# Gated linear attention followed by a two-layer network: step 2's loads placed behind the transfers into x, and the attention set at other units

## The chip, the cores and the metric

The kernel runs on 1 core of one Trainium2 chip. The metric is the device time of one execution in microseconds; the time given for the kernel before is the median of 3 runs. Shorter is better.

## The reference

For batch 4, 8 heads, 768 positions and a head size of 48, a state of 48 by 48 is carried along the positions; its 384 outputs per position then go through a two-layer network of width 2048.

```python
f = 1.0 / (1.0 + np.exp(-f_logit))
for t in range(S):
    state = f[:, :, t, :, None] * state + np.einsum('bhd,bhe->bhde', k[:, :, t], v[:, :, t])
    y[:, :, t] = np.einsum('bhd,bhde->bhe', q[:, :, t], state)
x = y.transpose(0, 2, 1, 3).reshape(B * S, H * D)
h = x @ w_in
g = np.where(h >= 1, h, np.where(h <= -1, 0.0, (h + 1) ** 2 / 4))
return g @ w_out
```

Inputs and outputs are float32.

## The kernel before, in words

The 768 positions are cut into 6 steps of 128 (step i = 0 to 5), all four batches at once, so that a step has 512 columns. In each step the attention gives x, 384 rows in three tiles `x[:, t]`, each as a rounded high part and a low part. The network then runs over 16 blocks j of 128 hidden rows.

**Units.** One block j of one step, 512 columns wide, is a unit. `unit_1` multiplies x by `w_in`: 9 matmuls into `ph` (high weight by both parts of x, then low weight, line 230). Its activation is made by ScalarE twice (lines 233 and 236), VectorE (line 241), ScalarE (rounding to `ghi`, line 244) and VectorE (the rest `glo`, line 247). `unit_2` multiplies by `w_out`: 9 matmuls into `po` (line 254). On TensorE `unit_2` of a unit comes after `unit_1` of the next. Units 0 to 15 are step 0. Step 1 starts in halves of 256 columns: units 16 to 19 are its first half of columns over blocks 0 to 7, two blocks each, units 20 to 23 the second half over the same blocks, and units 24 to 31 its blocks 8 to 15 at full width. From unit 32 on each step has 16 full units.

**Attention of a step.** It goes by four pairs of heads, n = 4i to 4i + 3. `gate` loads k and q (`in_kq`, 512 KB, line 267 through `dma`) and the gate logits (`in_f`), takes the sigmoid on ScalarE (line 443), runs two scans over the positions on VectorE (lines 445 and 452) and scales k and q (lines 454 and 456). `scores` is 16 matmuls of 128 columns (line 561) and a mask on VectorE (line 568). `outputs` (lines 622 and 630) gives two pairs of heads, rounded by ScalarE and VectorE (lines 600 and 601); `states` (line 670) carries the state on. The fourth pair's heads are made in a tile `y3` and moved into the three tiles of x by six small transfers, three on SyncE's queue (SP) and three on ScalarE's (line 272). `unit_1` of the step's first unit reads those rows. For step 1 this happens twice, once for each half of the columns; `moved[1, 1]` are the six transfers of its second half, which unit 20 reads.

**Weights.** They come as 64-bit words, in 24 pieces of 512 KB (`in_w`), and are put together by three VectorE operations each (`split_piece`, lines 335, 338 and 340) and split into a high and a low part, `w_hi` and `w_lo`. For 9 pieces, named by `moving`, the low part is made by ScalarE (line 345) and a transfer from GpSimd's queue that adds (line 346); for the other 15 by VectorE (line 350). Pieces are taken in the order `order[k]`: three of `w_in`, three of `w_out`, and so on, each group of six serving four units. All 24 pieces are read a second time later (`small_piece`, one reduction on VectorE each, line 358), only for a test on their size.

**What sets the order.** Every operation is given to a `Plan` with a cost and what it depends on; `Plan.order` then sorts all of them by a list schedule with these costs, and the engines get their instructions in that order. Dependencies in the plan set the order alone: the semaphores that an instruction waits for follow from the tiles that it reads and writes. Where the plan leaves TensorE idle for over 500 ns, `warm` puts in matmuls on zeros (line 308). `AT` and the table in the main loop say at which unit each `scores` (first list) and `outputs` (second list) is given to the plan.

Of the kernel before, what the change touches and what calls it, by code (L numbers as in the profile page):

```python
# [37 lines left out]
NT = 3  # L38

W = 512  # L40
NW = DM * DF // (128 * W)
# [99 lines left out]
def gla_moe(ctx: ExitStack, tc: tile.TileContext, ff, kqd, f0, vv, vad, vbd, wd, maskd, identd, gates, values, headsd, out):  # L141
# [30 lines left out]
    raw = tiles(3, [128, W], I64, "raw")  # L172
# [25 lines left out]
    HALVES = 1  # L198
# [67 lines left out]
    def dma(dst, src, kb, *deps):  # L266
        return add("SP", "issue", lambda: nc.sync.dma_start(dst, src), *deps, kb=kb)
# [46 lines left out]
    piece = []  # L314
# [9 lines left out]
    def split_piece(k):  # L324

        c = order[k]
        lw, hw = words_of(raw[k % 3])

        moving = k in (4, 6, 9, 10, 11, 12, 17, 19, 23)
        t = bits[k % 4]  # L330
        val = t.bitcast(F32)
        loaded = dma(raw[k % 3], wd[c], 8 * 128 * W / 1024, piece[k - 3] if k >= 3 else None)


        m = vec("words", lambda: nc.vector.tensor_scalar(
            out=t, in0=hw, scalar1=3, scalar2=0x3FFFFFF8, op0=ALU.logical_shift_left, op1=ALU.bitwise_and),
            loaded, split[order[k - 4]] if k >= 4 else None)
        v = vec("dve", lambda: nc.vector.scalar_tensor_tensor(  # L338
            out=t, in0=lw, scalar=29, in1=t, op0=ALU.logical_shift_right, op1=ALU.bitwise_or), m)
        v = vec("dve", lambda: nc.vector.scalar_tensor_tensor(  # L340
            out=t, in0=hw, scalar=0xC0000000, in1=t, op0=ALU.bitwise_and, op1=ALU.bitwise_or), v)
        piece.append(v)
        if moving:

            n = sca("copy", lambda: nc.scalar.activation(w_lo[:, c], val, AF.Copy, scale=-1.0), v)
            l = add("POOL", "swdge", lambda: nc.gpsimd.dma_start(w_lo[:, c], val, accum_op=ALU.add), n, kb=560)
            h = sca("copy", lambda: nc.scalar.copy(w_hi[:, c], val), v)
        else:
            h = sca("copy", lambda: nc.scalar.copy(w_hi[:, c], val), v)
            l = vec("dve", lambda: nc.vector.tensor_tensor(out=w_lo[:, c], in0=val, in1=w_hi[:, c].bitcast(F32), op=ALU.subtract), h)  # L350
        split[c] = [h, l]

    seen = []

    def small_piece(c):

        loaded = dma(raw[2], wd[c], 8 * 128 * W / 1024, seen[-1:] or piece[-3:])
        seen.append(vec("dve", lambda: nc.vector.tensor_reduce(
            out=ok[:, 1 + NG + c:2 + NG + c], in_=words_of(raw[2])[1].bitcast(F32), axis=mybir.AxisListType.X, op=ALU.min,
            apply_absolute_value=True), loaded))  # L360
# [30 lines left out]
    att = [None] * len(pairs)  # L391
# [4 lines left out]
    def old(n, *names, of=att):  # L396

        return [] if n < 0 else [of[n].get(k) for k in names]
# [7 lines left out]
    def gate(m, halves=(None,)):  # L406

        i, p = divmod(m, NT)
        t = kq[p]
        split_up = i == HALVES  # L410

        ft, before = (f[m], None) if m < 2 else (act_f[1], None) if m == 2 else (f[(m - 1) % 2], m - 3 if m < 5 else m - 2)
        et = end[m % 2]
        steps = ((0, 2), (2, 4)) if m == 0 or split_up else ((0, 4),)
        count = len(steps)
        if gates_of[m] is None:
            c = gates_of[m] = {k: [] for k in ("km", "qm", "sg", "en", "s2", "lf", "pf")}
            if not split_up:
                c["lk"] = dma(t[:, 0:2 * N], kqd[i, p], 512, [old(NP * i - k, "sc", "y", "tr") for k in ((1, 2, 3, 4) if i == HALVES + 1 else (NP - p,))],
                              old(m - NT, "km", "qm", "to", of=gates_of))  # L420
            else:
                c["lk"] = dma(t.rearrange("r (h c) -> r h c", h=2)[:, :, 0:N], kqd[i, p].rearrange("r (h c) -> r h c", h=2), 512,
                              old(NP * (i - 1) + p, "sc", "y", "tr"), old(m - NT, "km", "qm", "to", of=gates_of))
        c = gates_of[m]
        if m == 0:
            ready["mask"] = dma(mask, maskd, 64)
            ready["f0"] = sca(200, lambda: nc.scalar.activation(f0s, f0s, AF.Sigmoid), dma(f0s, f0, 36))
        lk = c["lk"]
        for h, (b0, b1) in enumerate(steps):
            if split_up and h not in halves:  # L430
                continue
            o = h if split_up else None

            shift = 1 if split_up and h else 0
            cols = slice(b0 * C + (1 if b0 and not split_up else 0) + shift, b1 * C + 1 + shift)
            l = dma(ft[:, cols], ff[i, p, :, cols], 256 // count, of_half(before, o, "qm") if before is not None else None)
            last = of_half(m - 1, o, "km", "en", "s2")
            u0, u1 = B - b1, B - b0
            fwd = ft[:, b0 * C + shift:b1 * C + shift]
            bwd = ft[:, b1 * C + shift:b0 * C + shift:-1]  # L440
            kt, qt = (t[:, HW * h:HW * h + HN], t[:, HW * h + HN:HW * h + 2 * HN]) if split_up else (
                wide(part(t, 0)[:, u0:u1]), wide(part(t, 1)[:, b0:b1]))
            sg = sca("sig" if count == 1 else 420, lambda cols=cols: nc.scalar.activation(ft[:, cols], ft[:, cols], AF.Sigmoid), l)  # L443

            s1 = vec(1200 // count, lambda bwd=bwd, u0=u0, u1=u1: nc.vector.tensor_tensor_scan(  # L445
                out=wide(w[:, u0:u1]), data0=bwd, data1=wide(ones[:, u0:u1]), initial=0.0,
                op0=ALU.mult, op1=ALU.add), sg, None if split_up else c["sg"], set_ones, last)
            en = vec("small", lambda b0=b0, b1=b1, u0=u0, u1=u1: nc.vector.tensor_scalar(
                out=et[:, b0:b1], in0=w[:, u1 - 1:(u0 - 1 if u0 else None):-1, C - 1], scalar1=1e-30, scalar2=None, op0=ALU.max),
                s1, of_half(m - 2, o, "pf"))  # L450
            rc = vec("small", lambda b0=b0, b1=b1: nc.vector.reciprocal(out=rec[:, b0:b1, 0], in_=et[:, b0:b1]), en, last, set_rec)
            s2 = vec(1200 // count, lambda fwd=fwd, b0=b0, b1=b1: nc.vector.tensor_tensor_scan(  # L452
                out=fwd, data0=fwd, data1=wide(rec[:, b0:b1]), initial=0.0, op0=ALU.mult, op1=ALU.add), rc, s1)
            km = vec(620 // count + 60 * (count - 1), lambda kt=kt, u0=u0, u1=u1: nc.vector.tensor_tensor(
                out=kt, in0=kt, in1=wide(w[:, u0:u1]), op=ALU.mult), s1, lk)
            qm = vec(620 // count + 60 * (count - 1), lambda qt=qt, fwd=fwd: nc.vector.tensor_tensor(
                out=qt, in0=qt, in1=fwd, op=ALU.mult), s2, lk)
            for name, d in (("sg", sg), ("en", en), ("km", km), ("qm", qm), ("s2", s2)):
                c[name].append(d)
            if split_up:  # L460
                least(m, h, t[:, HW * h + 2 * HN:HW * (h + 1)], et[:, b0:b1], f0s[:, m * B + b0:m * B + b1], en)
        if not split_up:
            least(m, None, whole(t), et, f0s[:, m * B:m * B + B], c["en"])
# [27 lines left out]
    def elementwise(n):  # L491
# [14 lines left out]
        if by_half:  # L506
            k = p % 2
            if h == 0:
                c["lv"] = dma(v[k], vv[i, k], 384, before, att[2]["st"])
            else:  # L510
                c["lv"] = att[n - 2]["lv"]
        elif n % 2:
            c["lv"] = att[n - 1]["lv"]
        elif i == 0:
            c["lv"] = dma(va if p == 0 else vb, vad if p == 0 else vbd, 512 if p == 0 else 640)
        else:
            c["lv"] = dma(v[k], vv[i, p // 2], 384, before, att[2]["st"])
        if NP - 1 in mine:

            every = range(NT * i, NT * i + NT)  # L520
# [318 lines left out]
        x_of[0, t] = rounded(firsts[t][0], wide(firsts[t][1]), x[0][:, t, 0], x[0][:, t, 1], y, None)  # L839
    for k in range(2 * NW):  # L840
        split_piece(k)
    for c in range(2 * NW):
        small_piece(c)

    BY_TENSOR = 2
    groups = {}

    AT = [5, 9, 16, 17], [10, 18]
    for n in range(NP, len(pairs)):
        i, m = divmod(n, NP)  # L850
        u = NJ * (i - 1)
        groups.setdefault(AT[0][m] if i == 1 else u + ((3, 4, 12, 13) if i == 2 else (-1, 0, 5, 10))[m], []).append((0, n))
        if m % 2 == 0:
            groups.setdefault(AT[1][m // 2] if i == 1 else u + ((7, 14) if i == 2 else (2, 13))[m // 2], []).append((1, n))
    for u in range(len(order_of)):
        unit_1(u)
        if u == 0:
# [15 lines left out]

        if 1 <= u < len(order_of) - 2:
            unit_2(u - 1)
    test()
    for u in range(len(order_of) - 3, len(order_of)):
        unit_2(u)
# [151 lines left out]
```

## Time and profile before

| | |
|---|---|
| runs | 511.97, 511.47, 509.25 us; median 511.47 us |
| the profiled execution | 514.73 us, of which the span from first to last instruction is 513.0 us |
| busy: TensorE | 498.4 us, 97% |
| busy: VectorE | 378.7 us, 74% |
| busy: ScalarE | 233.7 us, 46% |
| mean granted TensorE clock | 0.991 |
| DMA | 56.67 MB, mean 110 GB/s |

PE is TensorE, DVE VectorE, ACT ScalarE, POOL GpSimd and SP SyncE; a q behind a name is that engine's queue, where DMAs are issued. Times are microseconds from the span's start. In a timeline a row has start, length, engine, line, operation and tiles, and xN where N instructions are merged; in brackets stands the idle time of the engine just before and what ended it. Matmuls overlap each other, so that the distance between two starts says more than a length, and a busy PE is not one at its peak.

### The profile page before, as it was taken

The numbers are of one execution on the slowest core, as the hardware profiler recorded it, in microseconds if no ns is written. First come the engines' busy times: TensorE is split into PE (matmuls) and PEld (weight loads), VectorE is DVE, ScalarE is ACT, GpSimd is POOL, SyncE is SP. The second block draws the span as 40 slices with busy tenths as digits, with TensorE's granted clock in tenths as the row PEclk, the third lists the DMA queues.
The fourth block names the chain that finished last, engine by engine and source line by source line (L and its number), as shares of the span: only waits on it lengthen the run. The fifth ranks groups of instructions, "written<-read, shape, count | busy, mean of one in ns | idle before, by whom it ended". The sixth has DMA issues, their size and how long they took to land.

```text
span 513.0 us, 8673 instructions
## 1 busy us (share of the span) xinstructions
PE 498.4 (97%) x3412; PEld 406.1 (79%) x3412; DVE 378.7 (74%) x751; ACT 233.7 (46%) x386; POOL 31.9 (6%) x62
## 2 busy tenths in 40 slices
PE   8999999999799999999999999999999999999994
PEld 3677788789799877877888788788788888888883
DVE  7999999998689998999948999845755443433332
ACT  2266756653244443434543443543444444544441
POOL 2101301110100020101100010100000000000000
PEclk9999999999799999999999999999999999999999
DMA  8878947346504005230226150136533101100001
GB/s 314 248 242 280 251 143 203 115 124 211 186 2 145 1 21 145 108 99 0 74 92 165 66 183 18 46 124 174 184 125 123 42 1 31 64 0 1 0 1 67
DMA packets 21840, 56.67 MB, mean 110 GB/s; under 512 B 3456, under 2 KB 5120, under 8 KB 21792
## 3 DMA queue, kind: packets, MB, share of 16 engines
q1 hardware_dynamic: 19152, 51.51, 30.2%
q0 software_dynamic: 1296, 2.36, 2.6%
q10 hardware_dynamic: 1344, 2.17, 1.8%
q8 instruction: 29, 0.48, 0.4%
q14 instruction: 19, 0.16, 0.1%
HBM read 44.61 MB, written 4.72 MB: 96 GB/s over the span
## 4 chain that ended last, share of the span: by engine, by line
PE 53%; DVE 30%; DMA 9%; issue 3%; ACT 2%; SPq 1%; ACTq 0%; DVEq 0%
PE po L254 25%; PE ph L230 24%; DVE kn L595 7%; DVE act L241 3%; DVE glo L247 3%; DMA kq<-in_kq 3%; DVE am L568 3%; DVE bits L338 2%; PE pa L561 2%; DMA raw<-in_w 2%; DVE w L445 2%; DVE bits L340 2%; DVE f L452 2%; DMA v<-in_v 2%; DMA f<-in_f 2%
## 5 line engine op out<-in xcount | busy, mean ns | idle before, releaser
L230 PE MATMUL ph<-x,w_hi 128*128 128x512 f32 (+1 forms) x618 | 148.6, 376 | 3.2 <-DMA kq<-kq 3.1
L230 PEld LDWEIGHTS ph<-x,w_hi 128*128 128x128 f32 x618 | 111.8, 191 | 24.3 <-ACT ghi L244 3.3
L241 DVE SCALAR_TENSOR_TENSOR act<-ph,act 128x512 f32<-128x512 f32 x96 | 65.9, 687 | 79.9 <-ACT act L236 79.4
L233 ACT ACTIVATE act<-ph,half 128x512 f32<-128x512 f32 x96 | 66.0, 687 | 126.1 <-PE ph L230 110.3
L244 ACT CAST ghi<-act 128x512 fp32r<-128x512 f32 x96 | 59.5, 620 | 100.9 <-DVE act L241 95.9
L254 PE MATMUL po<-ghi,w_hi 128*128 128x512 f32 (+1 forms) x312 | 87.8, 388 | 1.0 <-ACT ghi L244 0.7
L247 DVE TENSOR_TENSOR glo<-act,ghi 128x512 fp32r<-128x512 f32 x96 | 65.8, 686 | 24.9 <-ACT ghi L244 23.7
L254 PE MATMUL po<-glo,w_hi 128*128 128x512 f32 (+1 forms) x312 | 83.6, 374 | 0.0
L254 PE MATMUL po<-ghi,w_lo 128*128 128x512 f32 (+1 forms) x312 | 83.6, 374 | 0.0
L230 PE MATMUL ph<-x,w_lo 128*128 128x512 f32 (+1 forms) x309 | 82.4, 375 | 0.7 <-DMA w_lo<-bits 0.7
L254 PEld LDWEIGHTS po<-ghi,w_hi 128*128 128x128 f32 x312 | 53.4, 188 | 15.4 <-ACT ghi L244 4.2
L230 PEld LDWEIGHTS ph<-x,w_lo 128*128 128x128 f32 x309 | 56.5, 191 | 11.3 <-DMA w_lo<-bits 1.1
L254 PEld LDWEIGHTS po<-glo,w_hi 128*128 128x128 f32 x312 | 55.6, 188 | 11.4 <-DVE glo L247 0.9
L254 PEld LDWEIGHTS po<-ghi,w_lo 128*128 128x128 f32 x312 | 55.9, 188 | 10.7
L236 ACT ACTIVATE act<-act 128x512 f32<-128x512 f32 x96 | 60.7, 632 | 4.0 <-issue 1.1
L595 DVE STREAM_TRANSPOSE kn<-kq 32x128 f32<-32x128 f32 x192 | 58.1, 302 | 2.8
L568 DVE TENSOR_TENSOR am<-pa,mask 128x512 f32<-128x512 f32 x46 | 30.2, 681 | 4.2 <-PE pa L561 4.2
L561 PEld LDWEIGHTS pa<-kq 48*128 48x128 f32 x368 | 24.1, 193 | 6.9 <-issue 5.0
L561 PE MATMUL pa<-kq 48*128 48x128 f32 x368 | 28.8, 291 | 0.0
L445 DVE TENSOR_TENSOR_SCAN w<-f,ones 128x512 f32<-128x512 f32 (+1 forms) x21 | 21.2, 1014 | 2.1 <-ACT f L443 2.1
L452 DVE TENSOR_TENSOR_SCAN f<-f,rec 128x512 f32<-128x512 f32 (+1 forms) x21 | 21.3, 1019 | 0.6
L443 ACT ACTIVATE f<-f 128x513 f32<-128x513 f32 (+2 forms) x21 | 11.3, 547 | 22.1 <-DMA kq<-kq 9.3
(88 smaller groups left out, 350.3 us busy)
## 6 DMA issues: line engine op xcount, KB each, us to landing
raw<-in_w SPq DMA_DIRECT2D x48, 512.0 KB, 3.9
kq<-in_kq SPq DMA_DIRECT2D x18, 512.0 KB, 5.3
out_y<-raw SPq DMA_DIRECT2D x18, 256.0 KB, 2.7
v<-in_v SPq DMA_DIRECT2D x10, 384.0 KB, 6.0
f<-in_f SPq DMA_DIRECT2D x13, 256.5 KB, 3.2
w_lo<-bits POOLq DMA_DIRECT2D x9, 256.0 KB, 5.0
kq<-kq SPq DMA_DIRECT2D x15, 64.2 KB, 4.8
kq<-kq ACTq DMA_DIRECT2D x15, 64.2 KB, 4.6
```

The costliest lines, as they stand in the source:

```text
L230: nc.tensor.matmul(ps[:, to], w_in(w_hi if high else w_lo, j, kt), xt[:, kt, t, c], start=(n == 0), stop=(n == 8))
L233: nc.scalar.activation(a, ps, AF.Relu, bias=half, scale=0.5)
L236: nc.scalar.activation(a, a, AF.Square)
L241: nc.vector.scalar_tensor_tensor(out=a, in0=ps, scalar=1.0, in1=a, op0=ALU.max, op1=ALU.min)
L244: nc.scalar.copy(hi, a)
L247: nc.vector.tensor_tensor(out=lo, in0=a, in1=hi.bitcast(F32), op=ALU.subtract)
L254: nc.tensor.matmul(po[e][:, c], w_out(part, j, e), g[:, of], start=(j == 0 and n == 0 and c.start == 0), stop=(j == NJ - 1 and n == 2))
L445: s1 = vec(1200 // count, lambda bwd=bwd, u0=u0, u1=u1: nc.vector.tensor_tensor_scan(out=wide(w[:, u0:u1]), data0=bwd, data1=wide(ones[:, ...
L452: s2 = vec(1200 // count, lambda fwd=fwd, b0=b0, b1=b1: nc.vector.tensor_tensor_scan(out=fwd, data0=fwd, data1=wide(rec[:, b0:b1]), initia ...
L561: nc.tensor.matmul(ps[:, m], key(n, q, b)[a:z], query(n, q, b)[a:z], start=True, stop=True)
L568: o = vec("dve", lambda t=t, ps=ps: nc.vector.tensor_tensor(out=t, in0=ps, in1=mask.rearrange("u (o t) -> u o t", o=1).broadcast_to([C, B, ...
L595: nc.vector.transpose(kn[n % 2][u:u + 32, ::-1, r:r + 32], src[:, :, u:u + 32])
```

## The change

Five things change. The loads of k and q for step 2 (`ahead` in `gate`) and every load of v from step 2 on (`elementwise`) get the six transfers `moved[1, 1]` as a dependency in the plan. So does the second reading of the weights (`small_piece`), which is also given to the plan after all units but the last instead of before the first. The list `moving` names other pieces, again 9. And the units at which scores and outputs are placed are others, for all of steps 1 to 5.

```diff
-        moving = k in (4, 6, 9, 10, 11, 12, 17, 19, 23)
+        moving = k in (4, 5, 7, 10, 11, 13, 17, 20, 21)
...
-        loaded = dma(raw[2], wd[c], 8 * 128 * W / 1024, seen[-1:] or piece[-3:])
+        loaded = dma(raw[2], wd[c], 8 * 128 * W / 1024, seen[-1:] or [piece[-3:], moved[HALVES, 1]])
...
+            ahead = moved[HALVES, 1] if i == HALVES + 1 else None
...
-                              old(m - NT, "km", "qm", "to", of=gates_of))
+                              old(m - NT, "km", "qm", "to", of=gates_of), ahead)
...
-            c["lv"] = dma(v[k], vv[i, p // 2], 384, before, att[2]["st"])
+            c["lv"] = dma(v[k], vv[i, p // 2], 384, before, att[2]["st"], moved[HALVES, 1])
...
-    AT = [5, 9, 16, 17], [10, 18]
+    AT = [3, 7, 14, 16], [10, 17]
...
-        groups.setdefault(AT[0][m] if i == 1 else u + ((3, 4, 12, 13) if i == 2 else (-1, 0, 5, 10))[m], []).append((0, n))
+        groups.setdefault(AT[0][m] if i == 1 else u + ((5, 8, 10, 12) if i == 2 else (-1, 2, 6, 8))[m], []).append((0, n))
...
-            groups.setdefault(AT[1][m // 2] if i == 1 else u + ((7, 14) if i == 2 else (2, 13))[m // 2], []).append((1, n))
+            groups.setdefault(AT[1][m // 2] if i == 1 else u + ((9, 13) if i == 2 else (4, 11))[m // 2], []).append((1, n))
```

Two lines are added ahead of the rest, so that from line 420 on a line of the changed kernel has a number higher by 2.

First, SP's queue around the transfers of step 1's second half into x (`x_86<-y_87`), before. `raw_92` and `raw_93` hold outputs of step 0, `kq_68` to `kq_70` get step 2's k and q, `raw_94` the second reading of the weights.

```order
L267 DMA out_y<-raw_93 128x512
L267 DMA raw_94<-in_w 128x512
L267 DMA kq_68<-in_kq 128x1024
L267 DMA kq_69<-in_kq 128x1024
L267 DMA kq_70<-in_kq 128x1024
L267 DMA v<-in_v 128x768 x2
L267 DMA raw_94<-in_w 128x512
L272 DMA x_86<-y_87 16x2x256 x3
L267 DMA f_67<-in_f 128x513
```

The same place of SP's queue in the changed kernel:

```order
L267 DMA out_y<-raw_93 128x512
L272 DMA x_86<-y_87 16x2x256 x3
L267 DMA kq_68<-in_kq 128x1024
L267 DMA kq_69<-in_kq 128x1024
L267 DMA v<-in_v 128x768
L267 DMA kq_70<-in_kq 128x1024
L267 DMA v<-in_v 128x768
L267 DMA raw_94<-in_w 128x512
L267 DMA f_67<-in_f 128x513
```

Seven large loads that stood ahead of SP's three transfers into x stand behind them or later. None of them has a semaphore of those transfers to wait for that it did not have: it is the place in the queue that changes.

Second, VectorE between line 241 of unit 12 (`act_83`) and of unit 13 (`act_84`), before:

```order
L241 SCALAR_TENSOR_TENSOR act_83<-ph_111,act_83 128x512
L350 TENSOR_TENSOR w_lo<-bits_96,w_hi 128x512
L338 SCALAR_TENSOR_TENSOR bits_98<-raw_94,bits_98 128x512
L247 TENSOR_TENSOR glo_90<-act_83,ghi_88 128x512
L340 SCALAR_TENSOR_TENSOR bits_98<-raw_94,bits_98 128x512
L350 TENSOR_TENSOR w_lo<-bits_97,w_hi 128x512
L601 TENSOR_TENSOR x_86<-pa_109,x_86 112x2x256
L241 SCALAR_TENSOR_TENSOR act_84<-ph_112,act_84 128x512
```

And in the changed kernel, without the first of these rows (lines 603, 456 and 458 are 601, 454 and 456 of before):

```order
L335 TENSOR_SCALAR bits_97<-raw_93 128x512
L603 TENSOR_TENSOR x_86<-pa_109,x_86 112x2x256
L247 TENSOR_TENSOR glo_90<-act_83,ghi_88 128x512
L458 TENSOR_TENSOR kq_68<-kq_68,f_66 128x256
L456 TENSOR_TENSOR kq_69<-kq_69,w 128x256
L458 TENSOR_TENSOR kq_69<-kq_69,f_67 128x256
L338 SCALAR_TENSOR_TENSOR bits_97<-raw_93,bits_97 128x512
L681 TENSOR_TENSOR sd<-pa_108,sd 112x4x96
L603 TENSOR_TENSOR x_86<-pa_110,x_86 112x256
L603 TENSOR_TENSOR y_87<-pa_110,y_87 112x256
L340 SCALAR_TENSOR_TENSOR bits_97<-raw_93,bits_97 128x512
L241 SCALAR_TENSOR_TENSOR act_84<-ph_112,act_84 128x512
```

Step 1's gates for its second half (456 and 458) and the rounding of its first half moved in ahead of unit 13's activation; two splits on line 350 moved out from between.

Third, TensorE in unit 12 (`ph_111<-x_85`) in the changed kernel, from its high weights to its low ones; before, the two L230 rows follow each other.

```order
L230 MATMUL ph_111<-x_85,w_hi 128x512 x6
L308 LDWEIGHTS zeros
L308 MATMUL po_115<-zeros 128x512
L308 LDWEIGHTS zeros
L308 MATMUL po_115<-zeros 128x512
L308 LDWEIGHTS zeros
L308 MATMUL po_115<-zeros 128x512
L308 LDWEIGHTS zeros
L308 MATMUL po_115<-zeros 128x512
L308 LDWEIGHTS zeros
L308 MATMUL po_115<-zeros 128x512
L230 MATMUL ph_111<-x_85,w_lo 128x512 x3
```

Five matmuls on zeros are put in there, and four more at the same place of unit 4; three that stood between units 5 and 6 are gone. In all there are 69 instead of 63.

More of the change, by code (lines that the diff above doesn't have):

```diff
@@ L841, in gla_moe @@
         split_piece(k)
-    for c in range(2 * NW):
-        small_piece(c)
     BY_TENSOR = 2
     groups = {}
-    AT = [5, 9, 16, 17], [10, 18]
+    AT = [3, 7, 14, 16], [10, 17]
     for n in range(NP, len(pairs)):
@@ L875, in gla_moe @@
             unit_2(u - 1)
+    for c in range(2 * NW):
+        small_piece(c)
     test()
```

## The prediction

> **What bounds the kernel now.** I read the page's head first, for the busy time of each engine and the strip of the clock.
>
> ```profile
> PE 498.4 (97%) x3412; PEld 406.1 (79%) x3412; DVE 378.7 (74%) x751; ACT 233.7 (46%) x386; POOL 31.9 (6%) x62
> PEclk9999999999799999999999999999999999999999
> ```
>
> PE is busy for 97% of the span, so that only what adds, removes or slows its work counts. In the strip one slice has a 7 where all others have a 9. The waits of PE (total, times, longest) say where it stands idle:
>
> ```profile
> PE ph L230 <- DMA kq<-kq: 3.1, 1, 3.1
> PE ph L308 <- DVE zeros L280: 1.7, 1, 1.7
> ...
> PE ph L230 <- DMA w_lo<-bits: 0.7, 1, 0.7
> ```
>
> One wait of 3.1 us stands out. PE's timeline around it shows the place:
>
> ```profile
> 126.83 0.88 PE L230 MATMUL ph<-x,w_hi 128*128 128x256 f32 x6
> ...
> 129.08 1.16 PE L561 MATMUL pa<-kq 48*128 48x128 f32 x16
> 130.17 0.98 PE L254 MATMUL po<-ghi,w_hi 128*128 128x256 f32 x6
> ...
> 135.68 1.84 PE L230 MATMUL ph<-x,w_hi 128*128 128x256 f32 x6 [3.08 <-DMA kq<-kq]
> ...
> 142.01 0.98 PE L254 MATMUL po<-ghi,w_hi 128*128 128x256 f32 x6
> ```
>
> The waiting matmuls read x, and they are unit 20's, the first of step 1's second half. PE had nothing to do from 135.68 − 3.08 = 132.60. Behind the wait, the same five groups (four of line 230, one of 561) that took 130.17 − 126.83 = 3.34 us at 126.83 take 142.01 − 135.68 = 6.33 us. Of the wait's 3.08 us the clock thus makes 3.08 + 2.99, about 6.1.
>
> The wait's releaser is given as a transfer `kq<-kq`, but what unit 20 reads is x. So I looked at SP's queue (start, length of the issues) around `moved[1, 1]`, with the first half's transfers for comparison, and at VectorE's row that makes y3 ready:
>
> ```profile
> 99.95 2.30 SPq L272 DMA_DIRECT2D x<-y  x3
> ...
> 121.47 1.34 SPq L267 DMA_DIRECT2D kq<-in_kq  x3
> 124.23 1.15 SPq L267 DMA_DIRECT2D v<-in_v  x2
> 125.48 0.51 SPq L267 DMA_DIRECT2D raw<-in_w  x1
> 127.56 4.26 SPq L272 DMA_DIRECT2D x<-y  x3
> ```
> ```profile
> 125.81 0.42 DVE L601 TENSOR_TENSOR y<-pa,y 112x256 fp32r<-112x256 f32 x1
> ```
> ```profile
> DMA to landing us min/median/max: 2.1/3.5/8.0
> ```
>
> y3 is ready at 125.81 + 0.42 = 126.23, SP issues its three transfers from 127.56 to 131.82, in 4.26 us against 2.30 for the first half, and the last row (tile x, SP's transfers) gives 3.5 us as their median from issue to landing. 131.82 + 3.5 = 135.3 meets PE's 135.68. Six large loads were issued in the 6 us before.
>
> The engine next to full is VectorE. Its share by stage (PE, PEld, DVE, ACT, POOL busy, then clock, DMA share, GB/s):
>
> ```profile
> 50.00:100.00 50.00, 49.90 (x321) 40.60 (x322) 49.28 (x97) 33.39 (x58) 8.47 (x11) 1.00 0.61 182
> 125.00:150.00 25.00, 21.91 (x169) 20.94 (x168) 17.78 (x39) 6.75 (x11) 1.31 (x2) 0.86 0.43 140
> 150.00:250.00 100.00, 99.41 (x758) 82.41 (x757) 95.66 (x216) 43.10 (x70) 7.82 (x12) 1.00 0.22 69
> ```
>
> From 50 to 100 VectorE has 0.7 us free in 50: whatever is put earlier in its order there makes something else later. From 125 to 150 it has 7.2 us free; the clock there is 0.86.
>
> **The change part by part.**
>
> *The x transfers.* Two things bring them forward. Large loads no longer stand ahead of SP's three, which should take the first half's 2.30 us. And the outputs go from unit 18 to 17, so that VectorE rounds y3 earlier: by order, one unit's operations of lines 241 and 247 and three small readings less stand ahead of it.
>
> ```profile
> L358 DVE TENSOR_REDUCE ok<-raw 128x1 f32<-128x512 f32 x24 | 16.4, 683 | 4.4 <-DMA raw<-in_w 4.3
> ```
>
> With the row's 683 ns for all five, which work on as many elements, that is 3.4 us; I take 3.0, since such operations overlap a little. y3 is then ready at 123.2, the issues end at 123.2 + 0.1 + 2.3 = 125.6, and x lands at 129.1 with the median of 3.5, at 133.6 with the greatest landing of 8.0. PE comes to unit 20 at 132.60, less the scores that move from unit 19 to 21 (129.08 to 130.17, 1.1 us), plus the 2.6 us by which it will be late (below): 134.1. The wait goes, with either landing. **−3.1 us for the wait, −3.0 us for the clock.** What is late next is nothing of x.
>
> *Warm matmuls and w_lo.* Nine are added, three taken away. Their price, and the piece transfers of line 346 with what unit 12 reads:
>
> ```profile
> 54.84 0.82 PE L308 MATMUL po<-zeros 128*128 128x512 bf16 x3
> 55.50 0.55 PE L581 MATMUL pa<-ident,kq 112*128 112x112 f32 x4
> ```
> ```profile
> 84.17 0.86 POOL L346 DMA_DIRECT2D w_lo<-bits  x1 [2.12 <-ACT w_lo L345]
> ```
> ```profile
> 90.97 0.84 PE L230 MATMUL ph<-x,w_lo 128*128 128x512 f32 x3
> ```
> ```profile
> DMA to landing us min/median/max: 3.8/5.0/7.9
> ```
>
> Three take 0.66 us from start to start, so six more are 1.3. Four of the nine take the place of the 0.7 us wait on `w_lo` at unit 4 (in the waits above): net +0.6. At unit 12 the low weight that arrives by transfer is piece 20's instead of 19's; issued about 1.5 us later than 84.17 (two and a half VectorE operations later by order), it lands at 89.5 to 93.6, against 90.97 plus five warm matmuls, 92.1. That is −0 to +1.5 us, median none.
>
> *Gates ahead of activations.* This is the part that costs. Of the second half's gates and rounding, by the order shown for VectorE, everything that ran from the first row 601 of 256 columns to unit 15's activation now stands ahead of unit 13's activation. In before:
>
> ```profile
> 94.33 0.68 DVE L241 SCALAR_TENSOR_TENSOR act<-ph,act 128x512 f32<-128x512 f32 x1
> ...
> 98.54 0.68 DVE L241 SCALAR_TENSOR_TENSOR act<-ph,act 128x512 f32<-128x512 f32 x1
> 99.14 0.41 DVE L601 TENSOR_TENSOR x<-pa,x 112x256 fp32r<-112x256 f32 x1
> ...
> 106.83 0.68 DVE L241 SCALAR_TENSOR_TENSOR act<-ph,act 128x512 f32<-128x512 f32 x1
> ```
> ```profile
> 99.25 0.62 ACT L244 CAST ghi<-act 128x512 fp32r<-128x512 f32 x1 [0.51 <-DVE act L241]
> ```
> ```profile
> 100.25 0.84 PE L254 MATMUL po<-ghi,w_hi 128*128 128x512 f32 x3
> ```
>
> Unit 13's is the row at 98.54. From 99.14 to 106.83 are 7.7 us; less three operations of the units themselves at 0.60 from start to start (98.54 to 99.14), 5.9. What moved out from ahead is one piece's three operations and two splits, five at 0.60 or a little less: 3.0. Unit 13's activation comes 2.9 us later by that. PE reads that unit's `ghi` at 100.25, 1.71 behind the row at 98.54; the activation (0.68) and ScalarE's rounding (0.62) with the passing on between them fill some 1.4 of that, so that 0.3 us is spare. PE is then 2.6 us late behind unit 13. The 0.6 us of warm matmuls and a wait for `w_lo` at unit 12 lie inside these 2.6, since PE would wait for VectorE anyway: the larger counts, not the sum. Later units gain nothing back on PE, which is full. **+2.6 us**; the ends are +0.6, if the order's extra work fits into pauses that I don't see, and +3.9, if nothing was spare and unit 15 sets it, ahead of which about 1 us more stands by order than ahead of unit 13.
>
> *Step 2's loads.* k and q go behind x.
>
> ```profile
> kq<-in_kq SPq DMA_DIRECT2D x18, 512.0 KB, 5.3
> ```
>
> Issued from 125.6 on instead of 121.47, and 5.3 us under way, they land some 4 us later, the first near 131, and VectorE waits that much for it. Their scores, however, go from unit 19 to unit 21, two units or 8 us later (94.33 to 98.54 is one), and VectorE has 7.2 us free there: nothing; with the cover gone at most the 4. The small readings that go back from here (four of them past 255 us, 2.7 us of VectorE) go to a stage where it has room; with them and the gates that moved, VectorE has about 3.6 us less ahead of unit 41 than before by order, which matches PE's gain. Nothing; if they collide, up to +2.
>
> The sum is −3.1 − 3.0 + 2.6 = **−3.5 us**. The profiled execution took 514.73 us (1.7 beside the span), so 511.2 by its own time. The median of the runs is 511.47, 3.3 under it; I take the difference over: **508.0 us**.
>
> **The rivals.**
>
> *The clock did not drop in ordinary runs (0.15).* The three runs spread from 509.25 to 511.97, 2.7 us, as much as the half clock costs, and the profiled one lies above them all; the two upper ones speak for a drop in most. Then only 3.1 goes and 2.6 comes: −0.5, 511.0. [...]
>
> *Slower: VectorE stops PE long enough (0.14).* If unit 13's lateness falls on PE in one piece of 3.1 us, the half clock moves from unit 20 to unit 13: 3.9 late there and 3.0 for the clock. Against it: 0.6 of it is filled by warm matmuls, and the 1.7 us wait above has no 7 in the strip. [...] Where the runs of before had the drop, this is −6.1 + 6.9 = +0.8; where they hadn't, −3.1 + 6.9 = +3.8, **515.3**. [...]
>
> *VectorE takes it back later (0.08).* At 95.66 of 100 us from 150 to 250 it follows PE closely; PE coming 3.5 us earlier may find activations unfinished. Against it stands the work moved back. Then about −0.5, 511.0.
>
> *The change doesn't do what it says (0.05).* No semaphore is added; ScalarE's three transfers into x keep their queue. If those are the late ones, and y3 is not earlier because VectorE is 2.9 us late, the wait stays and 2.6 comes: 514.1.
>
> **How the numbers follow.** The forecast has 0.58. Its own range comes from the 2.6: with +0.6, −5.5 or 506.0; with +3.9, −2.2 or 509.3. About 0.5%, 2.6 us, is what a measurement of this kernel can tell from no change, so faster means under 508.9. Of the forecast's 0.58, 0.52 lies there, with 0.02 of the first rival: 0.54 faster. The same: the forecast's upper end 0.06, 0.13, 0.08 and 0.02 of the last, 0.29. Slower: 0.14 and 0.03, 0.17. The range goes 1.5 below the forecast's end, for less VectorE work than PE's gain, and up over both rivals at 511.0 with 2 us for a wait on `w_lo` or a collision: 504.5 to 513.0.
>
> **What would show it.** Right: no wait before unit 20, no 7 in the clock's strip, the second half's L272 on SP issued within about 2.3 us and before kq; PE waiting for `ghi` at units 13 to 15, 1 to 2.5 us in all, with unit 20 at about 134. Wrong: a clock drop at another place, an idle at unit 20 left, or waits of PE on VectorE over 1 us between 150 and 290. If units 13 to 15 pass without a wait, the gain is 5.5; if their wait exceeds 3 us, the slower case has come.

## The result, and the profile after

| | before | after |
|---|---|---|
| median of the runs | 511.95 us (19 runs) | 508.46 us (19 runs, 507.01 to 509.35) |
| ratio to before | 1 | 0.9946, 95% interval 0.9928 to 0.9963 |
| the profiled execution | 514.73 us, span 513.0 | 509.32 us, span 507.4 |

The changed kernel is faster by 0.5%, some 2.8 us by the ratio and 3.5 by the medians. One of the 19 runs of before took 993.89 us and is left out of the ratio. The two profiled executions differ by more, 5.4 us; the run with the wait filled tells a part of why.

The head of the page of after: busy times, and the strip of the clock, which now has no 7.

```profile
PE 496.7 (98%) x3418; PEld 403.9 (80%) x3418; DVE 378.7 (75%) x751; ACT 236.0 (47%) x386; POOL 31.7 (6%) x62
PEclk9999999999999999999999999999999999999999
```

PE's waits of after. The wait of 3.1 us is gone, and so is the one on `w_lo`; what is new are short ones on VectorE and on the rounding by ScalarE.

```profile
PE ph L308 <- DVE zeros L280: 1.7, 1, 1.7
PE po L254 <- DVE glo L247: 1.2, 3, 0.5
PE po L254 <- ACT ghi L244: 0.7, 2, 0.5
PE po L563 <- issue: 0.2, 1, 0.2
```

SP's queue of after around `moved[1, 1]`, and VectorE's row that makes y3 ready:

```profile
123.33 1.90 SPq L272 DMA_DIRECT2D x<-y  x3
125.33 1.00 SPq L267 DMA_DIRECT2D kq<-in_kq  x2
```
```profile
122.85 0.42 DVE L603 TENSOR_TENSOR y<-pa,y 112x256 fp32r<-112x256 f32 x1
```

y3 is ready at 123.27, 3.0 us before its time in before, and SP gives out its three transfers in 1.90 us instead of 4.26. On PE, four rows of after tell what that was worth and what it cost:

```profile
102.41 1.16 PE L563 MATMUL pa<-kq 48*128 48x128 f32 x16
103.84 0.97 PE L254 MATMUL po<-ghi,w_hi 128*128 128x512 f32 x3 [0.27 <-ACT ghi L244]
...
126.70 0.88 PE L254 MATMUL po<-ghi,w_hi 128*128 128x256 f32 x6
...
133.18 0.88 PE L230 MATMUL ph<-x,w_hi 128*128 128x256 f32 x6
...
140.84 0.98 PE L254 MATMUL po<-ghi,w_hi 128*128 128x256 f32 x6
```

The row at 133.18 is unit 20's first group: it starts with no idle time before it, and 0.88 us long, at a granted clock of 1.00, where before it took 1.84 at 0.50. The row at 126.70 is `unit_2(17)`, ahead of which the same work stands in both kernels, but for the matmuls on zeros (nine instead of three). In before it started at the first of these rows; the second is `unit_2(20)`, in after the row at 140.84:

```profile
124.58 0.98 PE L254 MATMUL po<-ghi,w_hi 128*128 128x256 f32 x6
...
146.43 0.88 PE L254 MATMUL po<-ghi,w_hi 128*128 128x256 f32 x6
```

PE comes to `unit_2(17)` 2.1 us later than before, and to `unit_2(20)` 5.6 earlier, though with one group of scores (1.1 us) still to come. The row at 103.84 is unit 13's, where the forecast had PE waiting 2 us for VectorE. It waits 0.27: the scores of unit 14 (102.41) stand ahead of it in PE's order and fill the time, and PE is late already when it gets there. `unit_2(12)` starts at 97.74 (second row), against 96.17 in before (first row), with as many scores ahead of it. VectorE's activation of unit 13 (third row) starts 3.2 us later than its row at 98.54 in before.

```profile
96.17 0.84 PE L254 MATMUL po<-ghi,w_hi 128*128 128x512 f32 x3
```
```profile
97.74 0.92 PE L254 MATMUL po<-ghi,w_hi 128*128 128x512 f32 x3
```
```profile
101.77 0.69 DVE L241 SCALAR_TENSOR_TENSOR act<-ph,act 128x512 f32<-128x512 f32 x1
```

VectorE by stage in after (columns as before):

```profile
50.00:100.00 50.00, 49.45 (x307) 39.29 (x306) 49.07 (x96) 31.59 (x54) 7.91 (x12) 1.00 0.64 184
125.00:150.00 25.00, 25.00 (x216) 24.75 (x215) 18.24 (x39) 11.21 (x18) 1.31 (x2) 1.00 0.47 155
150.00:250.00 100.00, 99.69 (x761) 81.72 (x761) 96.83 (x217) 43.25 (x70) 6.89 (x12) 1.00 0.22 69
```

From 125 to 150 PE is busy for all of 25 us, at clock 1.00 instead of 21.91 at 0.86. From 50 to 100 it has 0.55 us idle instead of 0.10.

### The profile page after: what moved, and what is told of

Its sections match the earlier page's. It is cut to its first block, busy times and chain, and to the rows that moved or that the text cites. A ratio compares the mean times of both kernels' runs of the same rounds, so it can differ in the third digit from the quotient of the medians.

```text
span 507.4 us, 8656 instructions
## 1 busy us (share of the span) xinstructions
PE 496.7 (98%) x3418; PEld 403.9 (80%) x3418; DVE 378.7 (75%) x751; ACT 236.0 (47%) x386; POOL 31.7 (6%) x62
## 4 chain that ended last, share of the span: by engine, by line
PE 63%; DVE 24%; DMA 6%; issue 3%; ACT 2%; ACTq 0%; SPq 0%; POOL 0%; DVEq 0%
PE po L254 27%; PE ph L230 25%; DVE kn L597 6%; DMA raw<-in_w 4%; PE pa L563 3%; DVE glo L247 3%; PE ph L308 3%; DVE act L241 3%; PE pa L632 2%; DVE bits L338 2%; DVE am L570 2%; DVE bits L340 2%; PE pa L624 1%; DVE w L447 1%; DMA kq<-kq 1%
## 5 line engine op out<-in xcount | busy, mean ns | idle before, releaser
L230 PE MATMUL ph<-x,w_hi 128*128 128x512 f32 (+1 forms) x618 | 146.8, 373 | 0.0
L230 PEld LDWEIGHTS ph<-x,w_hi 128*128 128x128 f32 x618 | 110.6, 188 | 20.5
L230 PE MATMUL ph<-x,w_lo 128*128 128x512 f32 (+1 forms) x309 | 82.0, 374 | 0.0
L230 PEld LDWEIGHTS ph<-x,w_lo 128*128 128x128 f32 x309 | 55.9, 188 | 10.4
## 6 DMA issues: line engine op xcount, KB each, us to landing
raw<-in_w SPq DMA_DIRECT2D x48, 512.0 KB, 3.7
kq<-in_kq SPq DMA_DIRECT2D x18, 512.0 KB, 5.2
```

The costliest lines, as they stand in the source:

```text
L230: nc.tensor.matmul(ps[:, to], w_in(w_hi if high else w_lo, j, kt), xt[:, kt, t, c], start=(n == 0), stop=(n == 8))
```

## The experiments

The theory: six large loads ahead of SP's transfers, and y3 late by one unit, make x late, which costs a wait (3.08 us) and a half clock (0.50 granted behind it). The rivals: one of the two alone does it; the clock has nothing to do with it in ordinary runs. The change was taken apart into four parts, which the runs put together anew: the loads (with the second reading of the weights), step 1's units, the units of steps 2 to 5, and the list of pieces. The matmuls on zeros follow from the plan and differ with the parts. Each edit is shown against the kernel before or against the changed one, as said with it. Medians of before differed a little between the sets of runs (511.3 to 512.0), so that each ratio is against the runs of before on its own chip.

**The loads alone** (changed kernel with before's units, for all steps, and before's list).

```diff
-        moving = k in (4, 5, 7, 10, 11, 13, 17, 20, 21)
+        moving = k in (4, 6, 9, 10, 11, 12, 17, 19, 23)
...
-    AT = [3, 7, 14, 16], [10, 17]
+    AT = [5, 9, 16, 17], [10, 18]
...
-                if idle and o.start - idle > 500:
+                if idle and o.start - idle > 500 and o.start < 100000:
```

The plan would put matmuls on zeros into a wait that it sees here; the last line leaves them out, so that the wait can be seen.

> Only step 2's k, q and v and the second reading of the weights go behind the transfers into x; units of scores and outputs and the list of pieces as before. Theory: the six large loads ahead of SP's three transfers make x late. y3 is ready near 126.2 as before, SP issues in about 2.3 us, x lands by 132 and PE, which comes to unit 20 at 132.6, waits less than 0.5 us, with no half clock: the profiled span falls by about 6 from 513.0 to about 507, the median to 506 to 508.5. Rival: the earlier y3 is what helped; then PE still waits over 1.5 us at unit 20 and the time is within 1 us of before.

Measured: 513.44 us, ratio 1.0031 (1.0006 to 1.0056): slower than before. Neither theory nor rival had that. SP's queue and PE in this run:

```profile
125.18 1.95 SPq L272 DMA_DIRECT2D x<-y  x3
127.23 1.00 SPq L267 DMA_DIRECT2D kq<-in_kq  x2
```
```profile
133.50 2.04 PE L563 MATMUL pa<-kq 48*128 48x128 f32 x16 [4.79 <-DVE kq L458]
135.47 1.65 PE L254 MATMUL po<-ghi,w_hi 128*128 128x256 f32 x6
136.92 1.48 PE L254 MATMUL po<-ghi,w_lo 128*128 128x256 f32 x6
138.20 1.48 PE L254 MATMUL po<-glo,w_hi 128*128 128x256 f32 x6
139.48 1.30 PE L230 MATMUL ph<-x,w_hi 128*128 128x256 f32 x6
```

x is there: unit 20 (the row at 139.48) has no wait. But step 2's first scores still stand at unit 19, and k, q are now issued 6 us later than at 121.47. So PE waits 4.79 us one place ahead, for VectorE's scaling of kq, and the half clock follows as before (1.65, 1.48 and 1.48 us for groups that take 0.98, 0.88 and 0.88 from 143.23 on; mean clock 0.991). The loads cannot go back unless the scores that need them go back, too.

**The units alone** (kernel before with the new units of all steps).

```diff
-    AT = [5, 9, 16, 17], [10, 18]
+    AT = [3, 7, 14, 16], [10, 17]
-((3, 4, 12, 13) if i == 2 else (-1, 0, 5, 10))
+((5, 8, 10, 12) if i == 2 else (-1, 2, 6, 8))
```

and likewise for the outputs.

> Only the tables of units are the new ones; loads, second reading and list of pieces as before, so that six large loads still stand ahead of SP's transfers into x. Theory: y3 is ready 3 us earlier, but the issues still take over 4 us and x lands late by less than in before: a wait of 0 to 1.5 us at unit 20, no half clock, and the later units pay for VectorE's work that was put earlier: 508 to 511. Rival (the earlier y3 alone did it): no wait at unit 20, and the time is that of the changed kernel, 508.5 or less.

Measured: 509.29 us, ratio 0.9957 (0.9931 to 0.9982), inside the theory's range. A part of the rival holds: no wait at unit 20, though the loads stand where they did and SP still takes 5 us for three transfers.

```profile
119.25 1.68 SPq L267 DMA_DIRECT2D kq<-in_kq  x3
121.99 1.08 SPq L267 DMA_DIRECT2D v<-in_v  x2
123.37 5.41 SPq L272 DMA_DIRECT2D x<-y  x3
```
```profile
133.23 0.88 PE L230 MATMUL ph<-x,w_hi 128*128 128x256 f32 x6
```

The last issue ends at 128.78, 3 us before that of before, and PE comes later, at 133.23; both had a part in closing the gap. `unit_2(17)` starts at 126.75 here; this execution is 0.55 us early from the first unit on (35.52 against 36.07), so that PE is 2.7 us late. The plan has ten matmuls on zeros more here than in before; whether all of them lie inside waits, no run shows.

**The wait filled.** The kernel before, with 24 matmuls on zeros of 256 columns into `po[2]` ahead of unit 20:

```diff
+                if k == 20 and t == 0 and a == 0:
+                    for _ in range(24):
+                        nc.tensor.matmul(po[2][:, 0:HN], zeros, ..., start=False, stop=False)
```

> The kernel before, with 24 matmuls of 256 columns on zeros ahead of unit 20's first matmul, 2.9 us of work in a wait of 3.1; x comes as late as before. Theory: the wait costs twice, by itself and by the half clock behind it; with PE busy in it the clock stays, the five groups take 3.3 instead of 6.3 us, and the runs of before over 511 (some three in five of them) go: all near 509 to 510, median 509.3. Rival: the drop belonged to the profiled execution, or has another cause; then the times spread as before, median near 512.

Measured: 510.14 us (12 runs, 508.73 to 512.69), ratio 0.9981 (0.9959 to 1.0003).

```profile
131.62 2.79 PE L756 MATMUL po<-zeros 128*128 128x256 bf16 x24
134.17 1.10 PE L230 MATMUL ph<-x,w_hi 128*128 128x256 f32 x6
...
137.73 0.98 PE L254 MATMUL po<-ghi,w_hi 128*128 128x256 f32 x6
```

From 134.17 to 137.73 are 3.56 us for the five groups that took 6.33. All 12 runs have a mean clock of 0.996 or more. Of 91 runs of before on three chips, 36 have that, with a median of 510.08 us, and 55 have 0.995 or less, with a median of 512.48. The line between them is a choice: 12 runs have 0.995 itself, and 43 lie below it. So by the mean clock the half clock is in about half to three in five of the ordinary runs and goes with 2.4 us there, which makes about 1.5 on the average: theory and rival each have a part of it. That compares runs, whose waits are not on record; the run with the wait filled agrees, with a median 1.5 us under that of before on its chip, but its interval reaches 1. The profiled execution of before, at 0.991, is one of an extreme few: 4 of the 91 have 0.991 or less. The expected 509.3 was too low: times over 512 remain in this run without a drop of the clock, from something else.

**Without the nine matmuls on zeros** (changed kernel).

```diff
-                if idle and o.start - idle > 500:
+                if idle and o.start - idle > 500 and o.start < 40000:
```

> The changed kernel without the nine matmuls on zeros that units 4 and 12 have between their high and their low weights. Theory of the prediction: they lie inside what PE waits for anyway, so PE now waits 0.6 us on w_lo at unit 4, up to 1 us at unit 12 or as long on VectorE at unit 13, and the time is the same within 0.5 us; no idle near 3 us, so no half clock. Rival: they are plain work on PE; then 1 to 2 us less, 506.5 to 507.5.

Measured: 508.50 us, ratio 0.9943 (0.9918 to 0.9967), against the changed kernel's 508.46. As expected, PE waits instead, though not for `w_lo`:

```profile
PE po L254 <- ACT ghi L244: 2.2, 4, 0.7
PE ph L308 <- DVE zeros L280: 1.7, 1, 1.7
PE po L254 <- DVE glo L247: 0.8, 2, 0.5
```

The wait on the rounding has gone from 0.7 to 2.2 us. The nine matmuls lie inside what PE waits for anyway, and cost nothing that these runs can tell.

**Step 1's units alone** (kernel before).

```diff
-    AT = [5, 9, 16, 17], [10, 18]
+    AT = [3, 7, 14, 16], [10, 17]
```

> The kernel before with the new units for step 1 alone; loads, list of pieces and the units of steps 2 to 5 as before. Theory: y3 one unit earlier is by itself enough to take the wait at unit 20 away, with the loads ahead of it: no wait over 0.5 us at unit 20 and no half clock, PE some 2 us late from unit 13 on, 508.5 to 510. Rival: the units of step 2, too, had a part in what the run of the units showed; then a wait or a half clock is left near unit 19 or 20, 510.5 or more.

Measured: 512.06 us, ratio 1.0013 (0.9992 to 1.0033): no gain. The wait at unit 20 and the half clock are gone (clock 0.996 to 0.999 in all 12 runs), but the time is what it was. PE's waits from 136 to 260 us show where some of it went:

```profile
PE po L254 <- ACT ghi L244: 1.6, 3, 0.7
PE ph L230 <- DMA x<-y: 1.0, 3, 0.6
```

In the kernel before there are 0.3 us of them besides the wait at unit 20. PE comes 3.2 us earlier (`unit_2(19)` at 138.85 against 142.01) into the stage where VectorE is busy for 93.51 of 100 us (150 to 250), and with step 2's old units it waits there for activations and for step 2's x. That is the prediction's third rival, with old units for the later steps. The run of all units differs from this one by the later units alone, and there the gain is kept (0.9957 against 1.0013, on another chip).

**Loads and later units** (changed kernel with step 1's units and the list of before).

```diff
-        moving = k in (4, 5, 7, 10, 11, 13, 17, 20, 21)
+        moving = k in (4, 6, 9, 10, 11, 12, 17, 19, 23)
-    AT = [3, 7, 14, 16], [10, 17]
+    AT = [5, 9, 16, 17], [10, 18]
```

> Loads behind the transfers into x and the new units of steps 2 to 5; step 1's units and the list of pieces as before. Theory: the run of the loads alone failed because step 2's first scores stood at unit 19, ahead of what their loads allow; at unit 21 they have 8 us more, so neither they nor unit 20 waits over 0.5 us, no half clock, and since step 1's gates stay where they were PE does not come 2 us late behind unit 13: 506 to 507.5, under the changed kernel. Rival: PE still waits at unit 19, 20 or 21, or VectorE takes the 2 us back later: 508.5 or more.

Measured: 505.99 us, ratio 0.9893 (0.9862 to 0.9925). Once more, beside the changed kernel on one chip:

> The run with loads and later units once more, beside the changed kernel on one chip: 505.5 to 506.5, 1 to 3 us under the changed kernel, if keeping step 1's units and the old list saves PE's 2 us. Rival: no difference over 0.5 us between the two.

> The changed kernel again, for comparison on the same chip: 508 to 509.

Measured: 505.68 us, ratio 0.9900 (0.9870 to 0.9929), and for the changed kernel 508.27 us, ratio 0.9953 (0.9930 to 0.9976). The intervals do not touch: this version beats both kernels, the changed one by 2.6 us. In the trace of this second measurement VectorE's row for y3, SP and PE read:

```profile
124.81 0.41 DVE L603 TENSOR_TENSOR y<-pa,y 112x256 fp32r<-112x256 f32 x1
```
```profile
125.29 1.94 SPq L272 DMA_DIRECT2D x<-y  x3
127.33 2.08 SPq L267 DMA_DIRECT2D kq<-in_kq  x2
```
```profile
130.82 0.88 PE L230 MATMUL ph<-x,w_hi 128*128 128x256 f32 x6
...
137.39 1.16 PE L563 MATMUL pa<-kq 48*128 48x128 f32 x16
```

y3 is ready at 125.22, 1.0 us before its time in the trace of before and 2.0 after that of the changed kernel. The transfers are out by 127.23, and unit 20 starts without a wait at 130.82, 2.4 us before the changed kernel's 133.18. Step 2's first scores, at unit 21, do not wait either.

**The list alone** (kernel before).

```diff
-        moving = k in (4, 6, 9, 10, 11, 12, 17, 19, 23)
+        moving = k in (4, 5, 7, 10, 11, 13, 17, 20, 21)
```

> Only the list of the 9 pieces whose low part ScalarE and a transfer make is the new one. Theory: it moves nothing at unit 20, whose wait of about 3 us and half clock stay: 511 to 512.5, as before. Rival: the list carries part of the gain: 510 or less.

Measured: 512.39 us, ratio 1.0009 (0.9988 to 1.0030): the time is as expected, the reason isn't. All 12 runs have a clock of 0.996 or more, and there is no wait at unit 20 in the trace:

```profile
PE po L254 <- ACT ghi L244: 2.0, 5, 0.7
PE ph L308 <- DVE zeros L280: 1.7, 1, 1.7
PE po L254 <- DVE glo L247: 0.5, 1, 0.5
```
```profile
126.72 0.98 PE L254 MATMUL po<-ghi,w_hi 128*128 128x256 f32 x6
```

`unit_2(17)` starts at 126.72 against 124.58: the list makes PE 2.1 us late, and that lateness fills most of the wait at unit 20. PE waits 0.5 us for `glo` and 2.0 in five pieces for `ghi` (rows above), and the plan puts five matmuls on zeros into unit 12; how much of these waits stands ahead of `unit_2(17)`, and whether the five lie inside a wait, was not asked for the list alone. By the medians the list costs what it saves. Against the nine runs of before on its chip with a clock of 0.996 or more (median 510.25 us) it is 2.1 us slower, which the trace, of an execution of 510.67 us, does not explain.

**Without step 1's units** (changed kernel).

```diff
-    AT = [3, 7, 14, 16], [10, 17]
+    AT = [5, 9, 16, 17], [10, 18]
```

> The changed kernel with step 1's old units. Theory: as the run with loads and later units, with the list having little to say: 506 to 507.5, with PE less than 1 us late at unit 16 against before. Rival: step 1's units are needed for x to come in time; then a wait of 1 us or more at unit 20 and 509 or more.

Measured: 507.87 us, ratio 0.9931 (0.9907 to 0.9954). The time misses what was expected by 0.4 us, and PE's lateness does so clearly:

```profile
37.15 0.94 PE L254 MATMUL po<-ghi,w_hi 128*128 128x512 f32 x3
...
127.87 0.98 PE L254 MATMUL po<-ghi,w_hi 128*128 128x256 f32 x6
```

This execution is 1.1 us late from the first unit on (36.07 in the trace of before); less that, `unit_2(17)` is late by 3.29 − 1.08 = 2.2 us, as late as in the changed kernel. The list has much to say. In the changed kernel, which has step 1's units, too, it is 2.1, with the list alone 2.1, and with step 1's units but the old list 2.7: the two don't add. That both make PE wait for the same VectorE, busy for 49.07 of 50 us from 50 to 100 in the changed kernel, is the likely reason, and not shown. The time, 507.87 us, is 1.9 over that of the loads and later units on the same chip, from which this version differs by the list alone; no run of the one is as fast as any of the other.

**The later units alone** (kernel before).

```diff
-((3, 4, 12, 13) if i == 2 else (-1, 0, 5, 10))
+((5, 8, 10, 12) if i == 2 else (-1, 2, 6, 8))
```

and likewise for the outputs. Matmuls on zeros in the half-width stage are left out, as in the run of the loads alone.

> The kernel before with the new units of steps 2 to 5 alone; loads, list and step 1's units as before. Theory: with y3 as late as before, the six loads ahead of SP's transfers still make x late; PE, which has no scores at unit 19 now, comes a microsecond earlier to unit 20 and waits 3 to 4.5 us there, half clock in every run: 511 to 514. Rival: the units alone make the gain of the run with loads and later units; then no wait at unit 20 and 505.5 to 507.

Measured: 510.78 us, ratio 1.0001 (0.9980 to 1.0023). The median is a little under the range given; the wait is as the theory has it, the loads standing ahead of the transfers. The half clock in every run is not: the profiled execution does not have it (last section).

```profile
120.59 1.29 SPq L267 DMA_DIRECT2D kq<-in_kq  x3
...
125.34 4.81 SPq L272 DMA_DIRECT2D x<-y  x3
```
```profile
133.51 1.25 PE L230 MATMUL ph<-x,w_hi 128*128 128x256 f32 x6 [3.07 <-DMA x<-y]
...
134.96 0.88 PE L230 MATMUL ph<-x,w_hi 128*128 128x256 f32 x6
```

With the loads behind x, the same units gave 505.7 to 506.0. So with step 1's old units, and y3 ready at the same time in both traces (125.28 and 125.22), the place of the loads is worth 1%. With step 1's new units and the earlier y3 it is worth less: the changed kernel is only 0.8 us under the run of the units alone, from which it differs by the loads and the list, and the intervals do not tell the two apart.

**The loads alone, wait filled** (added to the run of the loads alone, where the plan sees the wait).

```diff
+                        for _ in range(36):
+                            nc.tensor.matmul(po[2][:, 0:HN], zeros, ..., start=False, stop=False)
```

> The run of the loads alone, with 36 matmuls of 256 columns on zeros (4.3 us) in the wait of 4.8 us ahead of step 2's first scores at unit 19. Theory: the wait stays, the half clock behind it goes (mean clock 0.996 or more in all runs instead of 0.989 to 0.992): 3 us less than that run, 510 to 511. Rival: the clock isn't what made that run slower than before; then 513 or more.

Measured: 511.61 us, ratio 1.0017 (0.9994 to 1.0041), clock 0.995 to 0.999 in all runs where it was 0.989 to 0.992. That is 1.8 us less by the medians than the loads alone, in the direction of the theory and less than its 3 us; the intervals overlap, and the size stays open.

## Why the prediction was right, and where it wasn't

The forecast was 508.0 us; the median is 508.46. Its steps, one by one:

- **x in time.** Right, and close in each number: y3 ready at 123.27 (forecast 123.2), the three issues 1.90 us long (2.3), unit 20 at 133.18 (134.1) without a wait. In eight traces with the loads behind them the three issues take 1.90 to 1.95 us, in six with the loads ahead 4.26 to 5.41. Which of the two reasons did it was not asked there. The runs say: the place of the loads is enough, if step 2's scores move, too (loads and later units), and it doesn't make PE late. The units alone take the wait away as well, but not by the earlier y3 only: PE is 2.7 us late there. Without that it would reach unit 20 at about 130.5, by estimate ahead of x, whose last issue ends at 128.78 and which would land at 132.3 with the median of 3.5 us of before.
- **The half clock, −3.0.** Right for the profiled execution, mis-sized for ordinary ones: by the mean clock it is in 43 to 55 of 91 runs of before and goes with 2.4 us there, so about −1.5 on the average. The rival that the clock did not drop in ordinary runs was thus half true. The working took one execution's clock over to the median, and that execution's clock was among the lowest of all.
- **Gates ahead of activations, +2.6.** Measured: +2.1 at `unit_2(17)`. On VectorE it came as foreseen: unit 13's activation is 3.2 us later (forecast 2.9). On PE the place was wrong: by the prediction's own sign PE should wait 1 to 2.5 us for `ghi` at units 13 to 15, and it waits 0.27. PE's order has the scores of unit 14 ahead of that place, which was overlooked, and 1.6 of the 2.1 us stand at `unit_2(12)` already, with five matmuls on zeros ahead of it in unit 12. And the cause was half seen. The list of pieces alone makes PE 2.1 us late, step 1's units with the old list 2.7, both together 2.1; the prediction looked at the list only for what arrives at unit 12. That the number came out near is thus in part luck.
- **Warm matmuls lie inside the wait.** Right: without them the time is the same (508.50 against 508.46), and the wait on the rounding grows by 1.5 us.
- **Step 2's loads, nothing; with the cover gone at most 4.** Right for the kernel, and the end was too low: with the scores left at unit 19 it is 4.79 us, and the half clock behind them, which was not counted there.
- **VectorE takes it back later.** Not in the changed kernel, whose windows from 150 to 250 have 0.31 us of idle PE against 0.59. It is what happens with step 1's units but without the later ones: then 2.6 us of waits appear and the gain is gone. The prediction gave the later units no share of the gain, only the cover for step 2's loads; they are what keeps it.
- **The end.** By the traces PE is 4.5 us ahead just behind unit 20 (5.6 at `unit_2(20)`, less the 1.1 us of scores that are still to come) and 5.4 at the end. Of these last 0.9 us, 0.3 are less idle from 150 to 250; the rest has not been traced.

So the sum was right in part because terms made up for each other: the clock gave 1.5 less on the average than was put down, lateness took 0.5 less, and 0.9 came later that nobody had forecast. The mechanism stands; the changed kernel reaches its gain by a way that gives 2.1 us back.

## What to carry to other kernels

A load that is moved behind something must have its first reader moved, too: here the loads alone made the kernel slower (1.0031) and the later units alone did nothing (1.0001), and only both together gave 1% (0.9893 and 0.9900). A wait further on hides lateness ahead of it: two parts that each made PE 2 us late or more looked free by the medians (1.0009 and 1.0013 of before, in which the wait stood). For the list the price, 1.9 us, shows once the wait is gone; for step 1's units without the list that was not run. When several parts are changed at once, run each without the others: the best version here is the change without two of its four parts.

## What the runs showed of the chip that was not expected

An idle of about 3.1 us of TensorE was followed by the half clock in one trace and not in another. The profile of before has 3.08 us, and a granted clock of 0.50 from 135.68 to 142.01 behind it. The profile of the later units alone has 3.07 us (the row at 133.51 above), and no half clock: its group of six behind the wait took 1.25 us, and every group of six from 134.96 to 139.28 took 0.88. That execution had a mean clock of 0.998; the 11 others of this kernel, whose idle times are not on record, had 0.989 to 0.995. The kernel with 4.79 us of idle in its profile had 0.989 to 0.992 in all 12 runs, and with the idle filled, none had less than 0.995.

The runs show a drop behind 3.08 us in one execution, none behind 3.07 in another, and a low mean clock in every run of the kernel whose profile has 4.79 us. What decided between the first two is not shown.
